# Linear attention and MoE mixer on one core: kv built transposed from split features, their column sums on GpSimd, four weight blocks reloaded in every batch

## The chip, the core and the metric

One core of a Trainium2 chip runs the whole kernel in one launch. The metric is the device time of that launch in microseconds. A core has TensorE (PE in the profile; its weight loads are PEld), VectorE (DVE), ScalarE (ACT), GpSimd (POOL) and SyncE (SP), which here only issues DMAs. TensorE reads SBUF and writes PSUM; VectorE and ScalarE read PSUM back.

## The reference

Eight batches, eight heads, 576 rows, head dimension 64, 128 features before the two signs:

```python
def phi(x):
    proj = np.einsum('bhsd,df->bhsf', x, w_phi)
    proj = proj - np.max(np.abs(proj), axis=-1, keepdims=True)
    return np.concatenate([np.exp(proj), np.exp(-proj)], axis=-1)
q_p, k_p = (phi(q), phi(k))
kv = np.einsum('bhsf,bhsd->bhfd', k_p, v)
z = np.sum(k_p, axis=2)
num = np.einsum('bhsf,bhfd->bhsd', q_p, kv)
den = np.einsum('bhsf,bhf->bhs', q_p, z)[..., None] + 1e-06
x = num / den          # then, with x as (batch, row, 512):
u = x + (xᵀ @ U @ V)ᵀ
out = u + np.maximum(u @ w_ch1, 0.0) @ w_ch2
```

The weights are float64 in memory and are turned into float32 on the chip.

## The kernel before

**Attention.** Work goes by pairs of heads: 4 pairs in a batch, 32 in all. Of the 576 rows, 512 go as four tiles of 128 (`NT`), and the last 64 of both heads as one "tail" tile. A `Pair` object has a step for each piece of the work: `s_project_k0` and `s_project_k1` (key features of each head, `kp`, 128 rows by 4 tiles by 256 features), `s_project_q0` and, inside `s_kv0_q1`, the second query head (query features `qp`, features by rows), `s_kv0_q1` and `s_kv1` (kv), `s_out0` and `s_out1` (queries times kv, then a division). In batches 0 and 1 (`split` false) everything runs in float32; from batch 2 on (`split` true, `SPLIT` is 2) the projections run in fp32r, a one-pass format, with operands split into a high and a low part. kv is float32 everywhere: `kv_tail` and `kv_main` hold the features as weights and stream v with a column of ones behind it (`vb`, 65 columns), so that column 64 of kv is z. `kv_done` copies kv from PSUM to SBUF. The features' maximum over 128 features is a VectorE reduction for k, and for q, whose features lie on partitions, a `partition_all_reduce` on GpSimd.

**MoE mixer.** A `Mixer` handles the 512 rows of a batch, and a ninth one the tails of all batches. It has 16 blocks f of 128 hidden columns: `hidden(f)` makes 12 fp32r matmuls of 512 columns into the one PSUM bank `ph`, ScalarE and VectorE split the result into `h_hi` and `h_lo` (L590, L591), and `add(f)` makes 12 more into the four banks `o`. All 32 weight tiles (`w1_f`, `w2_f`, high and low part, 512 KB each) stay in SBUF from their conversion (batches 0 and 1: `convert` on ScalarE, VectorE and, with `INT64_ADD`, GpSimd) to the end.

**Order.** The attention steps of the next pairs are woven with the 32 mixer chunks of the batch before: `mix` calls chunks between steps. A scheduler then sets the order of every engine's instructions by its own model of the time, and each engine keeps to that order. DMAs are all issued by SP, in its order. PSUM has 3 banks `at` for attention, 1 `ph` and 4 `o`. After the last pair only mixer chunks are left.

**What the change touches.** `load_weights`, `convert_block` and `place` name the weight tiles; `Pair.__init__` loads k and q; `project_k_split`, `project_q`, `kv_tail`, `kv_main`, `kv_done`, `out_main` and the steps `s_*` are those above; `hidden` and `add` are the mixer's.

## Time and profile before

| | |
|---|---|
| median of 3 runs | 1259.67 us (1258.68 to 1262.07) |
| profiled execution | 1257.95 us, span 1256.2 us |
| granted TensorE clock, mean | 0.991 |
| busy share of the span | PE 97%, PEld 83%, DVE 54%, ACT 43%, POOL 16% |
| chain that ended last | PE 84%, DVE 9%, ACT 4% |
| of that chain, by line | ph L585 30%, o L604 28%, kv L431 8%, xp L470 7% |

A row of a group of instructions reads: line, engine, operation, output <- inputs, shapes, count | busy us, mean ns of one | idle time of the engine before it and what ended that. Shapes are partitions x elements of one partition. A row of the order of time reads: start, duration, engine, line, operation, count. Matmuls are pipelined: each takes some 0.2 us longer than the step to the next, so a row's mean is not its price.

### The profile page before, as it was taken

How to read it: one execution, taken by the hardware profiler on the slowest of the kernel's cores; microseconds unless marked ns; L12 is line 12 of the kernel's file. 1: busy time of each engine (PE TensorE's matmuls, PEld its weight loads, DVE VectorE, ACT ScalarE, POOL GpSimd, SP SyncE). 2: the span in 40 equal slices, each digit the busy share in tenths (PEclk: the TensorE clock that was granted, in tenths of full speed). 3: DMA queues.
4: the chain of work that ended last, by engine and by line, in shares of the span. 5: the costliest groups of instructions: out<-in, count | busy, mean ns of one | idle time of the engine just before them, and what ended most of it. 6: DMA issues, size and time to landing. Idle time of an engine off the chain costs nothing.

```text
span 1256.2 us, 18188 instructions
## 1 busy us (share of the span) xinstructions
PE 1221.9 (97%) x6749; PEld 1044.6 (83%) x6749; DVE 680.5 (54%) x1489; ACT 541.6 (43%) x1151; POOL 204.0 (16%) x154
## 2 busy tenths in 40 slices
PE   7989998999999999999999999999999999999997
PEld 6877887888888888888888888888888888788886
DVE  5777889765566555565646556565646542212111
ACT  5766777444444444344434444344435430111110
POOL 3442444111110111011111111021101110000000
PEclk9899999999999999999999999999999999999999
DMA  5685111321132112311132112211222002100001
GB/s 125 210 254 176 65 28 29 100 63 27 32 87 62 25 29 58 93 30 29 29 100 62 23 34 64 80 30 27 45 78 63 17 1 88 67 1 1 34 1 33
DMA packets 188408, 75.42 MB, mean 60 GB/s; under 512 B 164256, under 2 KB 174752, under 8 KB 188192
## 3 DMA queue, kind: packets, MB, share of 16 engines
q1 hardware_dynamic: 188320, 74.27, 22.4%
q8 instruction: 53, 0.87, 0.3%
q14 instruction: 35, 0.29, 0.1%
HBM read 55.35 MB, written 18.87 MB: 59 GB/s over the span
## 4 chain that ended last, share of the span: by engine, by line
PE 84%; DVE 9%; ACT 4%; issue 1%; SPq 1%; DMA 1%; POOL 1%; DVEq 0%; ACTq 0%; POOLq 0%
PE ph L585 30%; PE o L604 28%; PE kv_ps L431 8%; PE xp L470 7%; PE pk L391 2%; PE pp L541 1%; DVE w L220 1%; PE kv_ps L424 1%; PE pq L414 1%; DVE uT_lo L228 1%; PE pt L573 1%; PE pq L415 1%; ACT w_ab L137 1%; ACT w_ab L138 1%; PE xpt L457 1%
## 5 line engine op out<-in xcount | busy, mean ns | idle before, releaser
L585 PE MATMUL ph<-uT_hi,w 128*128 128x512 f32 x1152 | 389.5, 398 | 2.3 <-ACT uT_hi L227 1.4
L604 PE MATMUL o<-w,h_hi 128*128 128x512 f32 x1152 | 330.7, 395 | 0.6 <-ACT h_hi L590 0.5
L585 PEld LDWEIGHTS ph<-uT_hi,w 128*128 128x128 f32 x1152 | 217.3, 189 | 48.9 <-ACT uT_hi L227 3.1
L604 PEld LDWEIGHTS o<-w,h_hi 128*128 128x128 f32 x1152 | 211.5, 188 | 42.5 <-ACT h_hi L590 1.2
L591 DVE SCALAR_TENSOR_TENSOR h_lo<-ph,h_hi 128x512 fp32r<-128x512 f32 x144 | 99.0, 687 | 256.5 <-ACT h_hi L590 256.1
L585 PE MATMUL ph<-uT_lo,w 128*128 128x512 f32 x576 | 227.3, 395 | 0.4 <-DVE uT_lo L228 0.4
L590 ACT ACTIVATE h_hi<-ph 128x512 fp32r<-128x512 f32 x144 | 85.9, 597 | 290.1 <-PE ph L585 281.3
L604 PE MATMUL o<-w,h_lo 128*128 128x512 f32 x576 | 198.0, 396 | 0.0
L355 POOL PARTITION_ALL_REDUCE qp<-qp x64 | 126.9, 1982 | 282.2 <-ACT qp L354 282.2
L431 PEld LDWEIGHTS kv_ps<-vb,kp 128*128 128x128 f32 x1024 | 126.0, 194 | 4.4 <-issue 1.4
L585 PEld LDWEIGHTS ph<-uT_lo,w 128*128 128x128 f32 x576 | 109.4, 190 | 22.2 <-DVE uT_lo L228 0.6
L470 PEld LDWEIGHTS xp<-kv,qp 128*128 128x128 f32 x1024 | 123.1, 192 | 5.4 <-ACT qp L358 1.0
L431 PE MATMUL kv_ps<-vb,kp 128*128 128x65 f32 x1024 | 125.1, 273 | 0.0
L470 PE MATMUL xp<-kv,qp 128*128 128x65 f32 x1024 | 123.2, 273 | 0.4 <-ACT qp L358 0.3
L604 PEld LDWEIGHTS o<-w,h_lo 128*128 128x128 f32 x576 | 105.6, 189 | 19.8
L355 POOL PARTITION_ALL_REDUCE qp_t<-qp_t x32 | 26.7, 834 | 433.6 <-ACT qp_t L354 433.6
L311 DVE TENSOR_TENSOR T<-raw,T 64x512 fp32r<-64x512 f32 x96 | 70.8, 737 | 29.3 <-ACT T L310 27.0
L345 ACT ACTIVATE kp<-kp 128x512 f32<-128x512 f32 x64 | 40.4, 632 | 103.8 <-DVE kp L342 71.5
L310 ACT CAST T<-raw 64x512 fp32r<-64x512 f32 x96 | 59.3, 618 | 29.2 <-PE pq L415 24.9
L357 ACT ACTIVATE qp<-qp 128x512 f32<-128x512 f32 x64 | 40.5, 632 | 66.2 <-DVE qp L356 65.8
L307 DVE STREAM_TRANSPOSE raw<-raw 128x512 f32<-128x512 f32 x48 | 34.1, 711 | 56.6 <-DMA raw<-in_q_dram 34.8
L146 POOL INT64_ADD w_ab<-w_ab x32 | 44.5, 1391 | 75.8 <-DVE w_ab L142 40.2
(127 smaller groups left out, 1371.3 us busy)
## 6 DMA issues: line engine op xcount, KB each, us to landing
words<-in_moe_w_ch_dram SPq DMA_DIRECT2D x32, 512.0 KB, 6.6
vb<-in_v_dram SPq DMA_DIRECT2D x64, 128.0 KB, 2.4
u_dram<-x SPq DMA_DIRECT2D x32, 256.0 KB, 2.6
st<-u_dram SPq DMA_DIRECT2D x16, 512.0 KB, 3.9
out_dram<-st SPq DMA_DIRECT2D x32, 256.0 KB, 2.2
raw<-in_k_dram SPq DMA_DIRECT2D x192, 32.0 KB, 1.9
raw<-in_q_dram SPq DMA_DIRECT2D x192, 32.0 KB, 1.9
raw<-in_k_dram SPq DMA_DIRECT2D x8, 256.0 KB, 2.9
```

What stands on the lines that cost most here:

```text
L146: nc.gpsimd.int64_add(a64, a64, b64)
L310: nc.scalar.copy(out=m[here, s, :], in_=x_[here])
L311: nc.vector.tensor_sub(m[there, s, :], x_[here], f32(m[here, s, :]))
L345: nc.scalar.activation(out=kp[:, :, 0:F], in_=kp[:, :, F:2 * F], func=AF.Exp)
L355: nc.gpsimd.partition_all_reduce(qp[:, 0, :], qp[:, 1, :], P, ReduceOp.absmax)
L357: nc.scalar.activation(out=qp[:, 0, :], in_=qp[:, 1, :], func=AF.Exp)
L431: nc.tensor.matmul(self.kv_v[:, f, g, :], kp[:, t, f * F:(f + 1) * F], self.vb[:, g, t, :], start=False, stop=(t == NT - 1), skip_group_ch ...
L470: nc.tensor.matmul(xv[:, c, :], qp[:, f, c * P:(c + 1) * P], self.kv[:, f, c // 2, :], start=(f == 0), stop=(f == 1))
L585: nc.tensor.matmul(ph, w1_part(f, l, c), r[:, c, :], start=(n == 0), stop=(n == 3 * NCC - 1))
L590: on_act = nc.scalar.activation(out=h_hi, in_=ph, func=AF.Relu)
L591: on_dve = nc.vector.scalar_tensor_tensor(out=h_lo, in0=ph, scalar=0.0, in1=f32(h_hi), op0=ALU.max, op1=ALU.subtract)
L604: nc.tensor.matmul(self.o[t], l[:, cs], w2_t[f][:, r, :], start=(f == 0 and n == 0), stop=(f == NFC - 1 and n == 2))
```

## The change

For the 24 pairs of batches 2 to 7:

- kv is built transposed. v is split into a high and a low part side by side (`v_parts`: 128 columns, which become the weights) and k's features into two parts (`k_parts`), and `kv_turned` streams both feature parts, 256 columns each in fp32r, past them: 8 matmuls a head. ScalarE and VectorE add the two halves of the result into `kvT`. At the head of the next turn of the loop, `kv_end` transposes kvT with two matmuls, adds it to the tail's kv, and puts z in.
- z no longer comes from the column of ones. `k_sums` adds the features over the partitions on GpSimd (128x1024 a head), SP stores one row of that in DRAM (`zd`), loads it back with features on partitions (`zc`, in pieces of 4 bytes), and `kv_end` reduces it on VectorE.
- SBUF for the parts comes from six weight tiles. Blocks 3, 7 and 11 no longer stay: after conversion, blocks 0, 3, 7 and 11 are written to DRAM (`kept`) from GpSimd's queue, and mixers 1 to 8 use block 0's place for the four in turn, reloading the next one behind the last use of the one before (`stream`, GpSimd's queue).

For the 8 pairs of batches 0 and 1, q is loaded in one DMA in place of four, and `project_q` makes each half from two matmuls that write every fourth element, so that a half is one head; `out_main` follows.

```diff
@@ weights
+    STREAM = (0, 3, 7, 11)
+    def place_of(n, f):
+        if f in STREAM[1:]:
+            return f"late{2 * STREAM.index(f) - 2 + n}"
+        return f"w{n + 1}_{f}"
+    def stream(n, g, f):
+        i = STREAM.index(f) + 1
+        to = STREAM[i % len(STREAM)]
+        if g == 0 or g == B and to == 0:
+            return
+        w = home.tile([P, 2, C], F32R, tag=place_of(n, 0), name=f"w{n + 1}_{to}_{g}")
+        nc.gpsimd.dma_start(out=w, in_=kept[to][:, n])
+        (w1_t, w2_t)[n][to] = w
...
+            if f in STREAM:
+                nc.gpsimd.dma_start(out=kept[f][:, n], in_=w)
@@ class Pair
-                elif n == 0:
+                else:
                     self.loaded = nc.sync.dma_start(
                         out=m, in_=src[b, hs, 0:SM, :].rearrange("h (p t) d -> p h (t d)", t=NT))
-                else:
-                    for g in range(2):
-                        for z in range(2):
...
+        def k_sums(self, g, kp):
+            zr = home.tile([P, NT, 2 * F], F32, tag="late2", name=f"zr{self.nm}_{g}")
+            nc.gpsimd.partition_all_reduce(zr, kp, P, ReduceOp.add)
...
+            nc.sync.dma_start(
+                out=self.zd[g:g + 1, :], in_=zr[0:1].rearrange("o t f -> o (t f)"))
+        def k_sums_turned(self):
+            self.zc = small.tile([P, 2, NT, 2], F32, tag="zc", bufs=2, name=f"zc{self.nm}")
+            nc.sync.dma_start(
+                out=self.zc.rearrange("p g t n -> p (g t n)"),
+                in_=self.zd.rearrange("g (t f) -> f (g t)", f=F))
+        def k_parts(self, g, kp):
...
+            nc.scalar.copy(out=hi, in_=kp)
+            nc.vector.tensor_sub(lo, kp, f32(hi))
+            return hi, lo
+        def kv_turned(self, g, parts):
+            kt = self.kt = self.ps(f"kt{g}_")
+            for t in range(NT):
+                for n in range(2):
+                    nc.tensor.matmul(
+                        kt[:, 0:2 * F], self.v_hl[:, g, t, :], parts[n][:, t, :],
+                        start=(t == 0 and n == 0), stop=(t == NT - 1 and n == 1))
...
+            nc.scalar.copy(out=self.kvT[r_, 1, :], in_=kt[D:2 * D, 0:2 * F])
+            nc.vector.tensor_add(self.kvT[r_, 0, :], kt[0:D, 0:2 * F], self.kvT[r_, 1, :])
+        def kv_end(self):
...
+            for f in range(2):
+                nc.tensor.transpose(
+                    out=kb[:, f * P:(f + 1) * P], in_=self.kvT[:, 0, f * F:(f + 1) * F],
+                    identity=ident)
+            self.kv_tail()
...
+            nc.vector.tensor_copy(out=self.kv, in_=self.kv_v)
+            nc.vector.tensor_add(
+                self.kv[:, :, :, 0:D], self.kv[:, :, :, 0:D],
+                kb.rearrange("p (f h d) -> p f h d", f=2, h=2))
...
         def project_q(self, s):
...
-                nc.tensor.matmul(pq, w_two[:, s, :], self.T[1], start=True, stop=True)
+                pv = pq.rearrange("f (p z i) -> f i z p", z=2, i=2)
+                for i in range(2):
+                    nc.tensor.matmul(
+                        pv[:, i], w_two[:, i, :],
+                        self.T[1][:, s * (SM // 2):(s + 1) * (SM // 2)], start=True, stop=True)
...
         def s_kv0_q1(self):
+            if self.split:
+                self.k_sums_turned()
+                self.kv_turned(0, self.parts0)
+                self.qp1 = self.project_q(1)
+                self.parts1 = self.k_parts(1, self.kp1)
+                return
@@ class Mixer, end of hidden(f) and of the matmuls of add(f)
+            if f in STREAM:
+                stream(0, self.g, f)
...
+            if f in STREAM:
+                stream(1, self.g, f)
@@ loop over pairs
+            cur.kv_end()
             far = Pair(*pairs[n + 2]) if n + 2 < len(pairs) else None
```

The built program shows where this puts the instructions. All places are in batch 5. TensorE before, around the first head's kv of the third pair (the names are output <- moving operand, weights; kv_ps is kv, pp the mixer's down projection, ph and o its blocks):

```order
L297 MATMUL tT_3_6880<-ident,t_r_3_6680 128x128
L424 MATMUL kv_ps_2_6916<-vt_90,kp_2_t 128x130 x2
L431 MATMUL kv_ps_2_6916<-vb_91,kp_2_0_6696 128x65
L541 MATMUL pp_0_6855<-xs_0_2_6820,u_all 128x256 x4
L541 MATMUL pp_0_6855<-xs_0_4_6825,u_all 128x256 x2
L431 MATMUL kv_ps_2_6916<-vb_91,kp_2_0_6696 128x65 x4
L585 MATMUL ph_5_6899<-uT_hi_6325,w_5_1376 128x512
```

TensorE now, where the second head's kv of that pair begins (kt is kv transposed, khi and klo the parts of the features):

```order
L709 MATMUL o_0_7123<-w_7_4_7414,h_lo_7_7665 128x512
L385 MATMUL kt_5_2_7491<-khi_2_1_7475,v_hl_2_7317 128x256
L709 MATMUL o_1_7124<-w_7_4_7414,h_lo_7_7665 128x512
L709 MATMUL o_2_7125<-w_7_4_7414,h_lo_7_7665 128x512
L709 MATMUL o_3_7126<-w_7_4_7414,h_hi_7_7664 128x512
L709 MATMUL o_3_7126<-w_7_4_7414,h_lo_7_7665 128x512
L385 MATMUL kt_5_2_7491<-klo_2_1_7476,v_hl_2_7317 128x256
L385 MATMUL kt_5_2_7491<-khi_2_1_7475,v_hl_2_7317 128x256
```

The 16 kv matmuls of 65 columns of a head have become 8 of 256 columns, which wait for the parts from ScalarE and VectorE.

The transposes of the same pair's kvT stand on TensorE 30 rows later, among the next pair's key projections (pk):

```order
L709 MATMUL o_0_7123<-w_8_1698,h_lo_8_7722 128x512
L709 MATMUL o_1_7124<-w_8_1698,h_lo_8_7722 128x512
L400 MATMUL kt_5_2_7491<-ident,kvT_2_7463 128x128 x2
L470 MATMUL pk_5_3_7565<-w_hl,T_5_3_7419 128x256 x2
L709 MATMUL o_2_7125<-w_8_1698,h_lo_8_7722 128x512
```

Before, kv ended with its last matmul of 65 columns; now these two stand between it and the first use.

GpSimd before, for the third and fourth pair of batch 5 (all are q's maxima; _t is the tail):

```order
L355 ISA qp_2_t<-qp_2_t 128x128
L355 ISA qp_2_0_6831<-qp_2_0_6831 128x512
L355 ISA qp_2_1_6930<-qp_2_1_6930 128x512
L355 ISA qp_3_t<-qp_3_t 128x128
L355 ISA qp_3_0_7131<-qp_3_0_7131 128x512
L355 ISA qp_3_1_7187<-qp_3_1_7187 128x512
```

GpSimd now, from the third pair's first query head on (zr are the sums over k's features, w the reloaded blocks 11 and 0 with their two tiles each):

```order
L211 DMA w_11_4_7668<-kept_107 128x1024
L434 ISA qp_2_0_7361<-qp_2_0_7361 128x512
L434 ISA qp_2_1_7469<-qp_2_1_7469 128x512
L211 DMA w_11_4_7783<-kept_107 128x1024
L353 ISA zr_3_0_7580<-kp_3_0_7564 128x1024
L434 ISA qp_3_t<-qp_3_t 128x128
L434 ISA qp_3_0_7698<-qp_3_0_7698 128x512
L353 ISA zr_3_1_7636<-kp_3_1_7620 128x1024
L211 DMA w_0_4_8030<-kept_104 128x1024
L434 ISA qp_3_1_7761<-qp_3_1_7761 128x512
L211 DMA w_0_4_8151<-kept_104 128x1024
```

Each reload waits for TensorE's last use of the block before it, and q's maxima stand behind reloads and sums.

SP before, for the loads of pair 1 of batch 5 (raw are the k and q loads, 8 DMAs each):

```order
L249 DMA raw_1_0_5968<-in_k_dram 32x8x32 x8
L269 DMA t_r_1_5986<-in_k_dram 64x2x64
L269 DMA t_r_1_5986<-in_q_dram 64x2x64
L283 DMA vt_96<-in_v_dram 64x64 x2
L280 DMA vb_97<-in_v_dram 128x4x64 x2
L249 DMA raw_1_1_5977<-in_q_dram 32x8x32 x8
```

SP now, for the same loads (zd is z's row in DRAM, zc its load back, here of the last pair of batch 4):

```order
L271 DMA raw_1_0_6412<-in_k_dram 32x8x32
L356 DMA zd_3_6170<-zr_3_0_6168 1x1024
L271 DMA raw_1_0_6412<-in_k_dram 32x8x32 x7
L283 DMA t_r_1_6430<-in_k_dram 64x2x64
L283 DMA t_r_1_6430<-in_q_dram 64x2x64
L356 DMA zd_3_6170<-zr_3_1_6224 1x1024
L271 DMA raw_1_1_6421<-in_q_dram 32x8x32 x2
L361 DMA zc_3_6332<-zd_3_6170 128x16x1
L271 DMA raw_1_1_6421<-in_q_dram 32x8x32 x6
```

The z stores, which wait for GpSimd, and the load back, which waits for the stores, stand inside the raw loads.

More of the change, by code (lines that the diff above doesn't have):

```diff
@@ L185, in tile_kernel @@
     LAST = NFC - 1
+    STREAM = (0, 3, 7, 11)
+    kept = {
+        f: dram.tile([P, 2, 2, C], F32R, name=f"kept{f}") for f in STREAM}
+    def place_of(n, f):
+        if f in STREAM[1:]:
+            return f"late{2 * STREAM.index(f) - 2 + n}"
+        return f"w{n + 1}_{f}"
     def place(f, dt, shape, name):
@@ L191, in place @@
             return both[:, 0], both[:, 1]
-        return [home.tile([P, *shape], dt, tag=f"w{n}_{f}", name=f"{name}_{n}") for n in (1, 2)]
+        return [home.tile([P, *shape], dt, tag=place_of(n, f), name=f"{name}_{n}") for n in (0, 1)]
+    def stream(n, g, f):
[6 more added lines that the diff above has]
+        (w1_t, w2_t)[n][to] = w
     def load_weights(f):
@@ L205, in convert_block @@
         if f < LAST:
-            w = home.tile([P, 2, C], F32R, tag=f"w{n + 1}_{f}", name=f"w{n + 1}_{f}")
+            w = home.tile([P, 2, C], F32R, tag=place_of(n, f), name=f"w{n + 1}_{f}")
             split_w((nc.scalar.copy, nc.vector.tensor_copy)[n], r, w)
+            if f in STREAM:
+                nc.gpsimd.dma_start(out=kept[f][:, n], in_=w)
         elif n == 0:
@@ L334, in k_tile @@
             return att.tile([P, ng, 2 * F], F32, tag=tag, bufs=bufs, name=f"kp{self.nm}_{n}")
+        def k_sums(self, g, kp):
+            zr = home.tile([P, NT, 2 * F], F32, tag="late2", name=f"zr{self.nm}_{g}")
+            nc.gpsimd.partition_all_reduce(zr, kp, P, ReduceOp.add)
+            if g == 0:
+                self.zd = dram.tile([2, NT * 2 * F], F32, tag="zd", bufs=2, name=f"zd{self.nm}")
+            nc.sync.dma_start(
+                out=self.zd[g:g + 1, :], in_=zr[0:1].rearrange("o t f -> o (t f)"))
@@ new lines, in k_sums_turned @@
+        def k_sums_turned(self):
[4 more added lines that the diff above has]
+        def k_parts(self, g, kp):
+            hi = home.tile([P, NT, 2 * F], F32R, tag=f"late{5 * g}", name=f"khi{self.nm}_{g}")
+            lo = home.tile([P, NT, 2 * F], F32R, tag="late1", name=f"klo{self.nm}_{g}")
+            nc.scalar.copy(out=hi, in_=kp)
+            nc.vector.tensor_sub(lo, kp, f32(hi))
+            return hi, lo
@@ new lines, in v_parts @@
+        def v_parts(self):
+            self.v_hl = home.tile([P, 2, NT, 2 * D], F32R, tag="late3", name=f"v_hl{self.nm}")
+            src = self.vb[:, :, :, 0:D]
+            nc.scalar.copy(out=self.v_hl[:, :, :, 0:D], in_=src)
+            nc.vector.tensor_sub(
+                self.v_hl[:, :, :, D:2 * D], src, f32(self.v_hl[:, :, :, 0:D]))
+        def kv_turned(self, g, parts):
[5 more added lines that the diff above has]
+                        start=(t == 0 and n == 0), stop=(t == NT - 1 and n == 1))
+            if g == 0:
+                self.kvT = home.tile([P, 2, 2 * F], F32, tag="late4", name=f"kvT{self.nm}")
+            r_ = slice(g * D, (g + 1) * D)
+            nc.scalar.copy(out=self.kvT[r_, 1, :], in_=kt[D:2 * D, 0:2 * F])
+            nc.vector.tensor_add(self.kvT[r_, 0, :], kt[0:D, 0:2 * F], self.kvT[r_, 1, :])
@@ new lines, in kv_end @@
+        def kv_end(self):
+            if not self.split:
+                return
+            kb = self.kt[:, 2 * F:4 * F]
+            for f in range(2):
[3 more added lines that the diff above has]
+            self.kv_tail()
+            self.kv = small.tile([P, 2, 2, D + 1], F32, tag="kv", bufs=1, name=f"kv{self.nm}")
+            nc.vector.tensor_copy(out=self.kv, in_=self.kv_v)
+            nc.vector.tensor_add(
+                self.kv[:, :, :, 0:D], self.kv[:, :, :, 0:D],
+                kb.rearrange("p (f h d) -> p f h d", f=2, h=2))
+            z = small.tile([P, 2, 2], F32, tag="z", bufs=2, name=f"z{self.nm}")
+            nc.vector.tensor_reduce(
+                out=z, in_=self.zc.rearrange("p g t n -> p n g t"), axis=AX.X, op=ALU.add)
+            nc.vector.tensor_add(
+                self.kv[:, :, :, D:D + 1], self.kv[:, :, :, D:D + 1], z.unsqueeze(3))
@@ L396, in project_k_split @@
                     out=k_w[:, ts_, :], in0=pk[:, :, 0, :], in1=kp[:, ts_, 0:F], op=ALU.add)
-            return self.k_features(g, k_w, kp)
+            self.k_features(g, k_w, kp)
+            self.k_sums(g, kp)
+            return kp
         def project_q_tail(self):
@@ L425, in kv_tail @@
                     self.kv_v[:, f, :, :], self.kpt[:, 0, f * F:(f + 1) * F], self.vt,
-                    start=(f == 0), stop=False, skip_group_check=True)
+                    start=(f == 0), stop=self.split and f == 1, skip_group_check=True)
         def kv_main(self, g, kp):
@@ L470, in out_main @@
                     nc.tensor.matmul(
-                        xv[:, c, :], qp[:, f, c * P:(c + 1) * P], self.kv[:, f, c // 2, :],
+                        xv[:, c, :], qp[:, f, c * P:(c + 1) * P],
+                        self.kv[:, f, c // 2 if self.split else s, :],
                         start=(f == 0), stop=(f == 1))
+            if not self.split:
+                h = self.h0 + s
+                self.normalize(s, xv, x[:, :, h * D:(h + 1) * D])
+                return
             xo = x.rearrange("p (s z) c -> p s z c", s=2)[:, s, :, self.h0 * D:(self.h0 + 2) * D]
@@ L493, in s_kv1 @@
         def s_kv1(self):
+            if self.split:
+                self.kv_turned(1, self.parts1)
+                return
             self.kv_main(1, self.kp1)
```

10 lines of the change are left out of this document (5 added, 5 removed).

## The prediction

> **What bounds the kernel now.** I read the page's head first, then the windows of the span, then the groups of instructions and the order of time on TensorE, and the waits last.
>
> ```profile
> span 1256.2 us, 18188 instructions
> PE 1221.9 (97%) x6749; PEld 1044.6 (83%) x6749; DVE 680.5 (54%) x1489; ACT 541.6 (43%) x1151; POOL 204.0 (16%) x154
> 0.00:62.80 62.80, 54.97 (x332) 45.34 (x333) 38.34 (x106) 42.13 (x96) 24.20 (x35) 0.95 0.58 167
> 188.40:219.80 31.40, 28.25 (x160) 23.58 (x158) 30.67 (x54) 24.76 (x50) 14.77 (x9) 1.00 0.16 29
> 400.00:970.00 570.00, 567.62 (x3248) 492.47 (x3248) 328.27 (x737) 251.93 (x550) 79.18 (x50) 1.00 0.22 50
> 970.00:1036.00 66.00, 66.00 (x386) 57.84 (x386) 31.82 (x81) 27.20 (x59) 9.46 (x6) 1.00 0.03 9
> L437 DVE COPY kv<-kv_ps 128x260 f32<-128x260 f32 x17 | 7.3, 427 | 13.5 <-PE kv_ps L431 13.5
> ```
>
> The window rows give the busy time of PE, PEld, DVE, ACT and POOL, then the granted clock and the DMA share. From 400 to 970 us TensorE lacks 2.4 us of 570, so there every matmul that goes is time that goes. The last row, of the same window, counts 17 head pairs, so a pair takes 570/17 = 33.5 us, and VectorE is busy for 328.27/17 = 19.3 us of it, ScalarE for 14.8. Only the first 62.8 us (7.8 us idle) and the weight conversion (188 to 220: VectorE busy 30.67 of 31.40, TensorE idle 3.2) are not bound by TensorE.
>
> **The kv matmuls.** The change touches the 24 pairs of batches 2 to 7.
>
> ```profile
> L431 PE MATMUL kv_ps<-vb,kp 128*128 128x65 f32 x1024 | 125.1, 273 | 0.0
> 402.66 2.57 PE L431 MATMUL kv_ps<-vb,kp 128*128 128x65 f32 x22
> 405.04 1.17 PE L604 MATMUL o<-w,h_hi 128*128 128x512 f32 x4
> 417.63 0.40 PE L391 MATMUL pk<-w_hl,T 128*128 128x256 f32 x2
> 417.86 0.40 PE L604 MATMUL o<-w,h_hi 128*128 128x512 f32 x1
> 435.70 0.96 PE L541 MATMUL pp<-xs,u_all 128*128 128x256 f32 x6
> 436.50 1.00 PE L431 MATMUL kv_ps<-vb,kp 128*128 128x65 f32 x8
> 402.11 0.27 PE L297 MATMUL tT<-ident,t_r 128*128 128x128 f32 x1
> 402.22 0.61 PE L424 MATMUL kv_ps<-vt,kp_t 128*128 128x130 f32 x4
> 440.75 0.48 PE L414 MATMUL pq<-T,w_hl 128*128 128x512 f32 x1
> 441.06 0.40 PE L415 MATMUL pq<-T,w_hl 128*128 128x512 f32 x1
> 441.30 0.63 PE L604 MATMUL o<-w,h_hi 128*128 128x512 f32 x2
> ```
>
> Matmuls overlap, so a price is the step from one start to the next. L431 has 1024 records for 32 pairs of 16 matmuls: an f32 matmul is two records. A record steps (405.04 - 402.66)/22 = 0.108 us. Removed: 24 x 32 = 768 records, 82.9 us. Added: 24 x 16 = 384 fp32r matmuls over 256 columns; fp32r rows of that shape step (417.86 - 417.63)/2 = 0.115 and (436.50 - 435.70)/6 = 0.133. I take 0.12, near the first, whose group is the purer one: 46.1 us (44.2 to 51.1). Two transposes of 128x128 a pair step like the one at 402.11, 0.11: 5.3 us. The first fp32r matmul behind f32 ones steps 0.31 (L414 at 440.75) and the next 0.24 (L415), 0.07 more; the order has 464 changes between the precisions before and 382 now, so 41 fewer of this direction: -2.9 us. Sum on TensorE: -82.9 + 46.1 + 5.3 - 2.9 = -34.4 us (-29 to -36).
>
> **What other engines get, a pair.**
>
> ```profile
> L591 DVE SCALAR_TENSOR_TENSOR h_lo<-ph,h_hi 128x512 fp32r<-128x512 f32 x144 | 99.0, 687 | 256.5 <-ACT h_hi L590 256.1
> L395 DVE TENSOR_TENSOR kp<-pk,kp 128x256 f32<-128x256 f32 x96 | 38.7, 417 | 13.2 <-ACT kp L394 13.0
> L354 ACT COPY qp<-pq 128x512 f32<-128x512 f32 x64 | 37.3, 583 | 14.9 <-PE pq L415 12.7 <-PE kv_ps L431 1.6
> L394 ACT COPY kp<-pk 128x256 f32<-128x256 f32 x96 | 34.5, 372 | 49.2 <-PE pk L391 48.9
> L355 POOL PARTITION_ALL_REDUCE qp<-qp x64: 1935/1939/2371, 14.1 to 1019.6; - x64
> 598.59 0.74 POOL L355 PARTITION_ALL_REDUCE qp_t<-qp_t  x1 [16.26 <-ACT qp_t L354]
> ```
>
> VectorE: 256 columns 0.417, 512 columns 0.687, so 1024 about 0.69 + 2 x 0.27 = 1.23. The low parts of k (2 x 1.23) and v (0.69), kvT (2 x 0.42), the add into kv (0.42) and two small ones (0.3) make 4.7 us: 24.0 of then 32.1 us, 75%. ScalarE: 2 x 1.0 for the high parts of k, 0.58 for v, 2 x 0.37: 3.3 us, 18.1 of 32.1. GpSimd: a reduction takes 0.74 at 128 columns and 1.94 at 512, so 3.5 at 1024, two of them: with q's, 2 x 1.94 + 0.74 + 7.0 = 11.6 us a pair, 36%. An addition in place of a maximum isn't in the trace; I bound it by 1.94 and 7 us. TensorE, the only full engine, hides all this as long as nobody is late.
>
> Late next would be the part behind ph: there is one ph bank, freed by L590 and L591, so VectorE can hold TensorE up if h_lo queues behind something that waits. Its new waits are for GpSimd (q's maximum now stands behind k's sums and the weight reloads), and, more often, for raw loads, which SP now issues between stores of z that wait for GpSimd.
>
> ```profile
> DVE raw L307 <- DMA raw<-in_q_dram: 34.8, 20, 3.5
> POOL qp L355 <- ACT qp L354: 282.2, 57, 9.3
> DVE qp L356 <- POOL qp L355: 4.4, 4, 2.3
> 425.41 0.40 PE L391 MATMUL pk<-w_hl,T 128*128 128x256 f32 x2
> 453.87 0.61 PE L457 MATMUL xpt<-kv,qp_t 128*128 128x130 f32 x4
> ```
>
> GpSimd mostly waits for its own input now (282.2 us for q alone), VectorE waits only 4.4 us in all for it, and raw loads already hold VectorE up for as much as 3.5 us without TensorE missing it. That cover I keep, in part: 0 to 1 us a pair lost (the conversion stretch loses 3.2 us of 31.4 with VectorE at 98%; at 75% it should be far less). I take 0.25 a pair, +6 us (0 to 24).
>
> z itself: the last key projection of the pair is at 425.41, and the first use of its kv at 453.87, 28 us. Between them stand an add like L395 for each half, a maximum, a subtraction and two exponentials over 512 columns of about L591's length (0.8 + 4 x 0.69 = 3.6 us), the sum (3.5), the store of z and its load back in 2048 pieces of 4 bytes. No row has such a load; by the rows of the next part, for 512 KB, the two take 8 to 13 us, 15 to 20 in all. Hidden, so zero, with 8 us for queues; if GpSimd is late by more than that, VectorE waits with h_lo behind it, which is rival A.
>
> **The reloads.** Eight of 512 KB a batch.
>
> ```profile
> words<-in_moe_w_ch_dram SPq DMA_DIRECT2D x32, 512.0 KB, 6.6
> st<-u_dram SPq DMA_DIRECT2D x16, 512.0 KB, 3.9
> 1113.39 2.72 PE ph L585 x12
> 1116.11 2.72 PE o L604 x12
> ```
>
> The shortest cover is in the last two mixers, where nothing lies between: hidden(1), add(0), hidden(2), add(1), 4 x 2.72 = 10.9 us from the last use of tile 0 to the first of tile 3; elsewhere 33.5/8 = 4.2 us a chunk, 16.8 us. Issue from GpSimd isn't in the trace; by the two DMA rows (3.9 to 6.6) and one 3.5 us reduction ahead of it, 4 to 10 us. Cost zero, with little to spare at the upper end. By the Trainium skill (DMA: Bandwidth & Descriptors, section on the anatomy of a SWDGE DMA) such a transfer takes about 2.0 us plus bytes/436 GB/s, estimated 3.2 us; the sum stays the same, and no run here shows that queue yet.
>
> **Start and conversion.**
>
> ```profile
> 1.23 1.99 SPq L260 DMA_DIRECT2D raw<-in_q_dram  x4
> 6.26 0.45 PE L297 MATMUL tT<-ident,t_r 128*128 128x128 f32 x1 [2.30 <-DMA t_r<-in_q_dram]
> 14.35 0.31 PE L297 MATMUL tT<-ident,t_r 128*128 128x128 f32 x1 [1.02 <-DMA t_r<-in_q_dram]
> L220 DVE TENSOR_TENSOR w<-w_ab,w x32: 644/692/1775, 62.5 to 235.7; 128x512 fp32r<-128x512 f32 x32
> L311 DVE TENSOR_TENSOR T<-raw,T x96: 684/686/1676, 187.0 to 992.3; 64x512 fp32r<-64x512 f32 x96
> ```
>
> q of batches 0 and 1 comes in one load in place of four (1.99 us), 1.5 us less of SP for each pair, and TensorE starts on the load behind it: -1.5 us at 6.26 and a part of 1.02 later (0 to -4). I take -2. The two half matmuls of q stream the same columns as the whole one: 0. Writing four tiles back, and pair (2,0)'s 4.7 us on a VectorE that is full from 188 to 220 us: 0 to +5, I take +2.
>
> Sum: -34.4 + 6 + 0 - 2 + 2 = -28.4 us, from the profiled execution's 1257.95 (span 1256.2): 1229.6. The median of the runs is 1259.67, 1.7 above, so I say 1231.
>
> **Rivals.**
> A, the cover is partly used up: waits of GpSimd and raw loads cost TensorE 0.6 to 1.25 us a pair in place of 0.25, 8 to 24 us more: 1239 to 1255. For it: VectorE rises to 75% and its queue is in order; against: 570 us with 2.4 us idle in spite of all waits now.
>
> B, VectorE becomes the bound and it gets slower. Instructions with two operands in SBUF are held up by a reduction on GpSimd: the slowest T is 1.676 us, 1.0 above its usual 0.686, and L220 likewise. If each of some ten such instructions a pair (T, q, the low parts) were held for 1 us, VectorE would need 34 of 32 us; TensorE then idles as at 188 to 220, 3.2 us in 31.4, over 24 pairs of 32.1 us 78 us: about 1309. It decides from 1.2 us a pair above my 0.25 on, 28 us in all, where nothing of the gain is left. Against: T's median is its minimum, so most aren't held. The Trainium skill (SBUF — State Buffer, section Who interferes with whom) says that the port pair of VectorE and GpSimd is locked for a whole instruction; by that rule a 3.5 us reduction holds such an instruction for up to 3.5 us, and the sum would be B's 1309 in place of 1231. The trace agrees that they collide, but shows at most half of a 1.94 us reduction.
>
> C, the reload is late: each of the eight mixers 1 to 8 then waits on tile 3, at 20 us of latency 2 x 9.1 + 6 x 3.2 = 37 us: 1268; at 19 us the gain is about gone. Against: 3.9 to 6.6 us in the rows.
>
> D, nothing gained: with new weights each time a 256-column matmul steps 0.20, or everything is lost to waits to within 4 us: 1260. Against: 0.133, the dearest step of such a run.
>
> **Numbers.** Forecast (1216 to 1238: the ends of the TensorE sum and of the start, -7, and some 0.3 us a pair of waits more, +7) 0.58; A 0.21; D 0.05; B 0.13; C 0.03. The range, 1216 to 1255, holds the first two. A measurement tells 0.3%, 3.8 us, from no change: faster 0.79, same 0.05, slower 0.16.
>
> **What would show it.** Right: the kv matmuls' 16 records a pair step 0.12, TensorE's busy time is some 34 us less, and the window of the middle batches stays within a few us of full. Wrong: TensorE idle before ph with h_lo as releaser (A, B); two-operand rows of VectorE at twice their time (B); TensorE waiting for a GpSimd DMA (C); kt steps of 0.2 (D); or a sum on GpSimd far over 3.5 us.

## The result and the profile after

The changed kernel takes 1401.1 us (median of four runs, 1393.8 to 1402.5) against 1259.2 for the kernel before: 1.112 times as long (95% interval 1.109 to 1.114). The forecast was 1231 us, faster. It was wrong in sign, and the time is far outside its range.

From the page of the changed kernel: its span, the busy time of the engines, the chain's shares, and then one row of the windows, the stretch of middle batches that the prediction read.

```profile
span 1398.7 us, 18303 instructions
PE 1256.1 (90%) x6443; PEld 1054.9 (75%) x6445; DVE 922.5 (66%) x1681; ACT 621.8 (44%) x1271; POOL 536.4 (38%) x272
PE 34%; DVE 32%; ACT 10%; DMA 8%; SPq 8%; issue 5%; POOL 2%; DVEq 0%; ACTq 0%; POOLq 0%
...
400.00:970.00 570.00, 495.47 (x2507) 414.34 (x2506) 415.62 (x731) 253.66 (x523) 246.59 (x96) 0.93 0.30 70
```

In the middle batches TensorE was idle for 2.4 us of 570; now it is idle for 74.5, and the granted clock is 0.93 in place of 1.00, so its busy time too holds slower matmuls. Of the chain that ended last, 32% lies on VectorE. No engine is full: the loss consists of waits, and of slower matmuls behind them.

The groups that grew, in the changed kernel (columns: busy us, mean ns of one, idle time before and its releasers), then the row of the kernel before that answers to L631, and two rows of the view by tile (shortest, median and longest, in ns).

```profile
L353 POOL PARTITION_ALL_REDUCE zr<-kp x48 | 295.0, 6145 | 196.7 <-ACT kp L425 167.2
L370 DVE TENSOR_TENSOR klo<-kp,khi 128x1024 fp32r<-128x1024 f32 x48 | 143.6, 2991 | 32.9 <-ACT khi L369 26.8
L325 DVE TENSOR_TENSOR T<-raw,T 64x512 fp32r<-64x512 f32 x96 | 79.8, 831 | 12.6 <-ACT T L324 9.7
L631 DVE TENSOR_TENSOR xs<-x,xs 128x256 fp32r<-128x256 f32 x64 | 67.2, 1090 | 9.7 <-ACT xs L630 9.6
```
```profile
L528 DVE TENSOR_TENSOR xs<-x,xs 128x256 fp32r<-128x256 f32 x64 | 29.1, 490 | 11.3 <-ACT xs L527 11.1
```
```profile
L370 DVE TENSOR_TENSOR klo<-kp,khi x48: 1181/3130/5553, 216.9 to 1172.2; 128x1024 fp32r<-128x1024 f32 x48
L353 POOL PARTITION_ALL_REDUCE zr<-kp x48: 6107/6114/6548, 216.4 to 1172.9; - x48
```

A sum on GpSimd takes 6.1 us, not 3.5. The same subtraction `klo` takes 1.18 us at its shortest, as the prediction estimated, and 5.55 at its longest. Sorted by what GpSimd did meanwhile, the nine `klo` that ran clear of GpSimd average 1.21 us and the 36 that lay at least 60% beside GpSimd's work 3.58; `xs` goes from 0.42 to 1.52. Operations with one operand in PSUM didn't change: the longest `h_lo` beside GpSimd's work is 0.69 us.

The moment at which a held operation ends is the clearest sign of what holds it. Of the `klo` that started during a sum, 28 took over 20% more than alone, and 27 of them ended 0.50 us before the sum's recorded end, whether they had started 0.5 or 4.2 us into it (the other one started in the sum's last 0.1 us and met the next reduction). The ten held `xs`, which need 0.8 us less, all ended 1.30 us before it. So each was let go 1.7 us before the sum's recorded end, as were four subtractions of q's maximum; those that started in its last 1.4 us were not held by it.

One such place in the order of time (start, duration, engine, line; in brackets the idle time before, and its releaser):

```profile
706.73 6.11 POOL L353 PARTITION_ALL_REDUCE zr<-kp  x1 [5.14 <-ACT kp L425]
706.82 1.89 PE L555 MATMUL xp<-kv,qp 128*128 128x65 f32 x16
707.67 4.66 DVE L370 TENSOR_TENSOR klo<-kp,khi 128x1024 fp32r<-128x1024 f32 x1 [1.74 <-ACT khi L369]
712.78 0.42 DVE L534 TENSOR_TENSOR x<-xp,den 128x256 f32<-128x256 f32 x1
713.35 0.30 PE L484 MATMUL pqt<-tail_T,w_hl 128*128 128x128 f32 x1 [2.95 <-DVE x L534]
713.60 3.26 PE L555 MATMUL xp<-kv,qp 128*128 128x65 f32 x16
```

The sum starts, `klo` starts behind it and takes 3.5 us more than alone, VectorE's queue (the division into `x`) stands behind it, and TensorE is idle for 2.95 us. Then it pays once more: 16 matmuls of L555 take 3.26 us where 16 such took 1.89 at 706.82, before the wait. The granted clock is 0.5 from 714.07 to 720.89 us.

The trace of the changed kernel has 27 such stretches at half the clock, 145 us in all. Before each but the last, which lies at the program's end, TensorE had been idle for at least 1.5 of the 3.4 us ahead of it. In these stretches matmuls of 512 columns are 0.43 us apart (median), elsewhere 0.23. That the idle time brings the lower clock on is what the order of events suggests; no run sets the two apart.

The longest waits of TensorE in total name VectorE (total us, times, longest of one); the wait of VectorE for z stands below them, then the row of the reloads, whose last figure is the time from issue to landing:

```profile
PE pt L676 <- DVE x L661: 21.9, 8, 5.5
PE pqt L484 <- DVE x L534: 18.8, 6, 4.0
PE ph L688 <- DVE h_lo L694: 15.2, 13, 1.4
```
```profile
DVE z L410 <- DMA zc<-zd: 41.9, 15, 4.7
```
```profile
w<-kept POOLq DMA_DIRECT2D x62, 512.0 KB, 4.1
```

No matmul waits for a reload, and the matmuls of kv step as forecast, with a median of 0.12 us:

```profile
733.39 0.28 PE L385 MATMUL kt<-klo,v_hl 128*128 128x256 f32 x1
733.51 0.28 PE L385 MATMUL kt<-khi,v_hl 128*128 128x256 f32 x1
```

### The profile page after: what moved, and what is told of

It is laid out like the page before. It is cut to its first block, busy times and chain, and to the rows that moved or that the text cites. A ratio compares the mean times of both kernels' runs of the same rounds, so it can differ in the third digit from the quotient of the medians.

```text
span 1398.7 us, 18303 instructions
## 1 busy us (share of the span) xinstructions
PE 1256.1 (90%) x6443; PEld 1054.9 (75%) x6445; DVE 922.5 (66%) x1681; ACT 621.8 (44%) x1271; POOL 536.4 (38%) x272
## 4 chain that ended last, share of the span: by engine, by line
PE 34%; DVE 32%; ACT 10%; DMA 8%; SPq 8%; issue 5%; POOL 2%; DVEq 0%; ACTq 0%; POOLq 0%
PE ph L688 12%; PE o L709 11%; DVE klo L370 8%; SPq L271 6%; DVE T L325 4%; PE xp L555 3%; DVE xs L631 2%; DVE mk L419 2%; DMA zc<-zd 2%; DVE h_lo L694 2%; DVE kp L474 2%; DVE kp L421 2%; DMA raw<-in_q_dram 2%; ACT khi L369 2%; ACT kp L424 1%
## 5 line engine op out<-in xcount | busy, mean ns | idle before, releaser
L353 POOL PARTITION_ALL_REDUCE zr<-kp x48 | 295.0, 6145 | 196.7 <-ACT kp L425 167.2
L709 PE MATMUL o<-w,h_hi 128*128 128x512 f32 x1152 | 338.3, 416 | 5.7 <-ACT h_hi L693 5.6
L709 PEld LDWEIGHTS o<-w,h_hi 128*128 128x128 f32 x1152 | 225.2, 201 | 54.9 <-ACT h_hi L693 9.2
L709 PE MATMUL o<-w,h_lo 128*128 128x512 f32 x576 | 188.4, 393 | 0.0
L211 POOL DMA_DIRECT2D w<-kept x62 | 34.3, 553 | 355.6 <-PE pk L470 144.5
L370 DVE TENSOR_TENSOR klo<-kp,khi 128x1024 fp32r<-128x1024 f32 x48 | 143.6, 2991 | 32.9 <-ACT khi L369 26.8
L555 PE MATMUL xp<-kv,qp 128*128 128x65 f32 x1024 | 136.8, 291 | 12.6 <-DVE kp L474 12.6
L555 PEld LDWEIGHTS xp<-kv,qp 128*128 128x128 f32 x1024 | 134.8, 208 | 17.3 <-DVE kp L474 13.7
L325 DVE TENSOR_TENSOR T<-raw,T 64x512 fp32r<-64x512 f32 x96 | 79.8, 831 | 12.6 <-ACT T L324 9.7
L631 DVE TENSOR_TENSOR xs<-x,xs 128x256 fp32r<-128x256 f32 x64 | 67.2, 1090 | 9.7 <-ACT xs L630 9.6
```

The source lines that it names most:

```text
L325: nc.vector.tensor_sub(m[there, s, :], x_[here], f32(m[here, s, :]))
L353: nc.gpsimd.partition_all_reduce(zr, kp, P, ReduceOp.add)
L370: nc.vector.tensor_sub(lo, kp, f32(hi))
L555: nc.tensor.matmul(xv[:, c, :], qp[:, f, c * P:(c + 1) * P], self.kv[:, f, c // 2 if self.split else s, :], start=(f == 0), stop=(f == 1))
L631: nc.vector.tensor_sub(xs[:, 1, :], src, f32(xs[:, 0, :]))
L709: nc.tensor.matmul(self.o[t], l[:, cs], w2_t[f][:, r, :], start=(f == 0 and n == 0), stop=(f == NFC - 1 and n == 2))
```

## The experiments

The theories. **Port** (later "lock"): a VectorE operation with two operands in SBUF stands still while a GpSimd reduction runs. **Load**: VectorE and ScalarE just have too much to do. **Queue** (later also "lateness"): z's chain, or what stands behind it on SP's or GpSimd's queue, comes too late. **Reload**: the four weight tiles come late. **Cover**: kv's cheaper products no longer hide the waits at a batch's end. All times are single runs unless more are given; single runs of the kernel before, on the same chips, lay between 1256.7 and 1262.2.

**The sum taken out**

```diff
-            nc.gpsimd.partition_all_reduce(zr, kp, P, ReduceOp.add)
...
-                out=self.zd[g:g + 1, :], in_=zr[0:1].rearrange("o t f -> o (t f)"))
+                out=self.zd[g:g + 1, :], in_=kp[0:1].rearrange("o t f -> o (t f)"))
```

> The changed kernel without the sum of k's features on GpSimd: the store of z takes a row of the features themselves, so z is left out of the result, and everything else (parts, kt matmuls, transposes, store and load back of z, reloads) stays. Port theory (the 6.1 us sum reads SBUF and holds VectorE's instructions with two SBUF operands; VectorE runs late, TensorE idles): 1225 to 1245 us, klo near 1.2 us in place of 3.0. Queue theory (the long sum makes q's maxima and z late): also 1225 to 1245. Load theory (VectorE's 4.7 us of new work a pair is too much by itself): over 1330. Reload theory (GpSimd's queue and DMAs for the weight tiles): over 1330.

Measured: 4655.85 us, which no theory had. The row of TensorE's first work, products on zeros ahead of any data:

```profile
1.23 7.95 PE L812 MATMUL busy<-zeros 128*128 128x512 bf16 x6 [1.23 <-DVE zeros L807]
```

Six of them take 7.95 us; in the changed kernel 2.74. So TensorE was slower by a factor of about 3 from the first instruction, at a granted clock of 1.0 in the records, before anything of the change could matter; `klo` on VectorE took its usual 1.22 us. The run says nothing of the sum, and I repeated it (the step of these products in the changed kernel is 0.43 us, not the 0.22 that the text below says):

> The kernel of the first experiment a second time: the sum over partitions on GpSimd is gone, zd is stored from kp's first row, so the output lacks the true z; everything else of the change stays (the store and the load that turn z, the kv in feature layout, the reloads, q's whole loads). In the first run TensorE needed 1.3 us for each of the six 128x512 products on zeros that open the program, where after needs 0.22 between starts, so nothing of the change could have come into it yet. If that was a disturbance of that one run, the time is now 1220 to 1260 us by the lock theory (VectorE's klo back to 1.2 us everywhere, xs to 0.42) and by the lateness theory alike (no 6.1 us in z's chain); by the load theory (VectorE has too much to do) it stays above 1300. If 4656 us comes again, the cause is in this program and not in the chip's state.

Measured: 1259.4 us, with `klo` at 1.22 us on average and `xs` at 0.51.

```profile
PE 1197.4 (95%) x6443; PEld 1021.4 (81%) x6445; DVE 781.2 (62%) x1681; ACT 619.9 (49%) x1271; POOL 246.8 (20%) x224
L368 DVE TENSOR_TENSOR klo<-kp,khi 128x1024 fp32r<-128x1024 f32 x48 | 58.8, 1224 | 29.7 <-ACT khi L367 28.1
```

So the sum is worth 141 us of the changed kernel's time. On TensorE these are 82 us more of idle time and 59 us more of busy time for the same matmuls (the table at the end of the experiments). VectorE's busy time also differs by 141 us, but that is a coincidence as far as the runs show, since TensorE did not wait for all of it. Load falls as the main cause: VectorE still does all its added work here. What made the first run slow stays open. Also open was why 1259 is still 28 us above the forecast; see "batch ends" below.

**GpSimd as busy, but without reading** (a sum over 128x128 and four memsets; z is not the true one)

```diff
-            nc.gpsimd.partition_all_reduce(zr, kp, P, ReduceOp.add)
+            nc.gpsimd.partition_all_reduce(zr[:, 0, 0:F], kp[:, 0, 0:F], P, ReduceOp.add)
+            for _ in range(4):
+                nc.gpsimd.memset(zr, 1.0)
```

> GpSimd is kept busy for about as long as by the sum, without reading SBUF for most of it: each sum is replaced by one over 128 columns (0.7 to 1 us) and four memsets of 128x1024, together some 5 to 6 us; z is left out. Port theory: klo back to 1.2 to 1.6 us, 1230 to 1265 us. Queue theory: as slow as the changed kernel, 1370 to 1400.

Measured: 1325.6 us. Its groups, and its longest wait of SP's queue:

```profile
L355 POOL MEMSET zr<- 128x1024 f32 x192 | 185.4, 965 | 8.4
L372 DVE TENSOR_TENSOR klo<-kp,khi 128x1024 fp32r<-128x1024 f32 x48 | 58.5, 1219 | 45.0 <-ACT khi L371 44.6
...
SPq L358 <- POOL zr L355: 345.1, 31, 19.7
```

GpSimd works 4.95 us for each head, and `klo` runs at its own 1.22 us: the memsets, which only write SBUF, don't hold it. The Trainium skill (SBUF — State Buffer, section Who interferes with whom) says just that: two SBUF operands contend with a GpSimd instruction that reads SBUF, not with one that only writes it. But 66 us over the kernel without a sum are left, with VectorE's operations no slower than there (`xs` 0.45 against 0.51 us, `T` 0.74 against 0.72): GpSimd's time costs in a second way (the last experiment).

**A shorter reduction** (the maximum in place of the sum; z is not the true one; the instructions stand in the same order as in the changed kernel)

```diff
-            nc.gpsimd.partition_all_reduce(zr, kp, P, ReduceOp.add)
+            nc.gpsimd.partition_all_reduce(zr, kp, P, ReduceOp.absmax)
```

> The sum becomes a maximum of absolute values of the same 128x1024, in the same instruction order; z is left out. By the rows of q's maxima (0.74 us at 128 columns, 1.94 at 512) it takes 3.5 us if the operation sets the price, and 6.1 if the size does. Port theory and queue theory: with 3.5 us the time falls by about half of what is lost, to 1290 to 1340; with 6.1 it stays at 1400. Load and reload theories: 1400 either way.

Measured: 1302.6 us.

```profile
L353 POOL PARTITION_ALL_REDUCE zr<-kp x48 | 171.2, 3568 | 192.2 <-ACT kp L425 141.9
L370 DVE TENSOR_TENSOR klo<-kp,khi 128x1024 fp32r<-128x1024 f32 x48 | 87.5, 1823 | 34.2 <-ACT khi L369 29.8
```

The maximum takes 3.57 us, which is the 3.5 that the prediction worked out for the sum: from the maxima of q it had the price of a maximum, and an addition costs 1.72 times that. 124 us less of GpSimd are 98 us less of time, with every engine's instructions in the same order: nothing but the length of the reduction differs. Even at 3.5 us the kernel would have been slower than before, so the mis-sized sum alone does not explain the forecast's error.

**The reloads alone**, in the kernel before (blocks 0, 3, 7 and 11 written back once and reloaded; nothing else of the change)

> The kernel before with the reload of weight tiles alone (blocks 0, 3, 7, 11 written to DRAM and reloaded by mixers 1 to 8 on GpSimd's queue; kv, z and the loads of q as before). Port and queue theories: 1255 to 1266 us. Reload theory: 1290 or more, with TensorE waiting for the tiles or GpSimd's maxima late.

Measured: 1256.1 us, the kernel before beside it 1257.1. A reload lands in 4.3 us. Reload falls, and the cost of zero was right.

**z not waited for** (sum, store and load stay; kv's last column is added from a constant, so z is not the true one)

```diff
-                out=z, in_=self.zc.rearrange("p g t n -> p n g t"), axis=AX.X, op=ALU.add)
...
+                self.vb[:, :, 0:2, D:D + 1])
```

> The sum on GpSimd, its store and its load stay as they are, but nothing waits for them on VectorE: z is added from a constant (v's column of ones) in place of zc, so the output lacks the true z. By the lock theory the 6.1 us sums still stop klo (3 us mean) and xs (1.1 us mean), and at most the 42 us that VectorE waited for zc can go: 1350 to 1395 us. By the lateness theory (z's chain of sum, store and load comes too late for kv) the time falls to 1230 to 1290 us with klo's mean still at 3 us.

Measured: 1388.7 us, with `klo` at 2.89 us on average. VectorE's wait of 42 us for z was worth some 12 us (5 against the fastest run of the changed kernel); lateness of z falls as the main cause.

**The same sum in four instructions**

```diff
-            nc.gpsimd.partition_all_reduce(zr, kp, P, ReduceOp.add)
+            for t in range(NT):
+                nc.gpsimd.partition_all_reduce(zr[:, t, :], kp[:, t, :], P, ReduceOp.add)
```

> The same sum in four instructions of 128x256 in place of one of 128x1024; the same numbers come out. By the lock theory (VectorE's operations with two operands in SBUF wait until the running GpSimd instruction lets go) klo under GpSimd falls from 3.6 us to 1.5 to 2.8, since it waits for a quarter at most, and the time falls by 20 to 110 us to 1290 to 1380, though GpSimd works as long as before (four times 1.6 to 2 us against 6.1). By the load theory and by the lateness theory the time is 1390 to 1430 us, as GpSimd's sums last as long or longer.

Measured: 1329.2 us.

```profile
L354 POOL PARTITION_ALL_REDUCE zr<-kp x192 | 366.9, 1983 | 217.0 <-ACT kp L426 184.8
L371 DVE TENSOR_TENSOR klo<-kp,khi 128x1024 fp32r<-128x1024 f32 x48 | 65.9, 1372 | 27.2 <-ACT khi L370 19.6
```

GpSimd works 72 us longer, on the same numbers, and the kernel is 72 us faster: what counts is how long one instruction keeps VectorE out. It speaks for the lock, since load and lateness could only have grown.

**z without GpSimd** (a reduction over kp's four tiles on VectorE, four products with the column of ones on TensorE; no store, no load; four runs)

```diff
-            nc.gpsimd.partition_all_reduce(zr, kp, P, ReduceOp.add)
+            nc.vector.tensor_reduce(
+                out=self.zs[:, g, :], in_=kp.rearrange("p t f -> p f t"), axis=AX.X, op=ALU.add)
...
+                        self.kv_v[:, f, g, D:D + 1], self.zs[:, g, f * F:(f + 1) * F],
+                        self.vb[:, g, 0, D:D + 1],
```

> z without GpSimd and without the two transfers: VectorE adds kp's four tiles (one tensor_reduce of 128x1024 to 128x256 for a head, estimated 1.2 us from klo alone, 1.21), and TensorE adds four products with v's column of ones to kv's tail (four at 0.11 us). The rest of the change stays. Priced on the forecast's terms: 1231 us, plus 24 x 0.44 = 10.6 on TensorE, plus 2.4 us of VectorE a pair that is hidden if the lock was the cause: 1230 to 1265 us. By the load theory (VectorE's work for a pair, 24 of 32 us and now 26, is what stalls TensorE) it is above 1300 us.

Measured: 1285.2 us, 1.020 times the kernel before (1.017 to 1.024). The expectation missed two prices: the reduction takes 2.02 us, not 1.2, and a float32 product is two records on TensorE, so z costs some 20 us there, not 10.6. The same with two additions in place of the reduction:

> The kernel with z on VectorE and TensorE (1285 us), with two additions (128x512 and 128x256, estimated 0.69 and 0.42 us from the additions of the same sizes) in place of the one reduction, which measured 2.00 us: 0.9 us less for a head, 43 us less of VectorE over the program; the same z. If VectorE's work in a pair still costs time there at the rate of the last step (from no z, 1259, to this z, 1285, with 96 us more on VectorE and 10.6 on TensorE: 26 us), half of the added VectorE work goes and 7 to 12 us with it: 1271 to 1279 us. If that 26 us is TensorE's 10.6 and the batch ends, nothing: 1281 to 1290.

Measured: 1276.4 us, 9 less, inside the first of the two ranges; the additions take 0.76 and 0.44 us. It is one run, so how much of VectorE's work counts in full isn't settled by it.

**Batch ends.** In the kernel without the sum TensorE still waits in one place, in the order of time at the end of a batch:

```profile
385.08 0.71 DVE L321 STREAM_TRANSPOSE raw<-raw 128x512 f32<-128x512 f32 x1 [2.88 <-DMA raw<-in_q_dram]
386.29 2.47 DVE L726 TENSOR_TENSOR st<-st,o 128x512 f32<-128x512 f32 x4
388.68 1.28 DVE L659 TENSOR_TENSOR x<-x,vp 128x512 f32<-128x512 f32 x2
389.41 1.97 PE L674 MATMUL pt<-ident,x 128*128 128x128 f32 x8 [5.42 <-DVE x L659]
```

VectorE waits 2.88 us for q's load, other work and `x` stand behind it in its order, and the next mixer's transposes wait 5.42 us for `x`. Two experiments on the kernel without the sum (so without the true z), and a control on the kernel before. First, two chunks of the mixer more held back for the end of a batch, `HELD = 4` made 6:

> The kernel without the sum (1259.4 us) with one number changed: six mixer chunks in place of four are held back for the end of each batch (HELD), about 5.6 us more of TensorE work there. The kernel without the sum still stands 28 us above the forecast, and its TensorE waits 26 us for VectorE's x at the six ends of batches (PE pt from DVE x, 5.4 us the longest). Theory cover: kv's one-pass products took away what TensorE did at the end of a batch, so the wait of VectorE for q's load is uncovered there; then two chunks more cover it and the time falls by 10 to 28 us, to 1231 to 1249, with that wait below 10 us. Theory rate: VectorE's and ScalarE's added work slows every pair alike, and the time stays 1255 to 1265 us.

Measured: 1238.3 us, 21 less; TensorE's wait for `x`, first without and then with the two chunks:

```profile
PE pt L674 <- DVE x L659: 25.9, 6, 5.4
PE pt L674 <- DVE x L659: 10.6, 6, 1.8
```

The control, the kernel before with HELD 6:

> The kernel before with the same number changed (HELD 6). Control: its TensorE never waits for x at a batch's end (no such row among its waits), so by the theory cover nothing is to be had there: 1255 to 1265 us. If it gains as much as the kernel without the sum does, the held chunks are a gain of their own and say nothing of the change.

Measured: 1258.8 us (beside it 1261.2): nothing to be had there beyond what two single runs differ by. So the change uncovered the wait at the batch ends. Whether kv's cheaper products did it, as the theory says, or VectorE's added work, which also makes `x` later, isn't set apart. Then the order of the steps that fill the end of a batch:

```diff
-                    fill = [nxt.s_project_q0, far.transposes, nxt.s_kv0_q1, nxt.s_kv1]
+                    fill = [nxt.s_project_q0, nxt.s_kv0_q1, far.transposes, nxt.s_kv1]
```

> The kernel without the sum, with the next-but-one pair's transposes moved behind the first kv product in the list of steps that fill a batch's end, so that VectorE meets the wait for q's load one step later. By the theory that VectorE stands in its own order in front of a late load with x queued behind, the wait of TensorE for x falls from 26 us to below 13 and the time by 8 to 25 us, to 1234 to 1251; if the wait only moves to another row, 1255 to 1265.

Measured: 1252.4 us, 7 less, the wait 9.6 us. The sign and the wait are as expected, the gain just short of the range.

And the changed kernel itself with HELD 6, sum and true z included:

> The changed kernel, sum on GpSimd and all, with HELD 6. By the lock theory VectorE stands still in every pair (24 times two sums of 6.1 us), which 5.6 us of TensorE work at a batch's end cannot cover: the time falls by no more than the 21 us that the kernel without the sum gained, to 1378 to 1401 us. By the theory that the sum only lengthens the batch ends, it falls to 1300 or lower.

Measured: 1390.8 us. Held chunks win 10 us here: the sum's price lies mostly in every pair, not at the batch ends.

**Is there a version that wins?** z by two additions with HELD 6 (four runs):

> z by two additions on VectorE and four products on TensorE (1276 us) with HELD 6; the outputs are those of the reference. From the gain of the kernel without the sum (21 us): 1276 - 21 = 1255, and a little lower if the 12 us that are left over TensorE's own 10.6 for z also lay at the batch ends: 1243 to 1258 us, against about 1259 for the kernel before. If it stays above 1265, VectorE's work is the bound in every pair and not only at the ends.

Measured: 1272.4 us, 1.011 times the kernel before (1.009 to 1.013), above the expected range. The expectation would lay that on VectorE's work in every pair. By the traces, of the 34 us between this kernel and the one without the sum and with HELD 6, 25 are busy time of TensorE, z's products and slower matmuls, and 8 its idle time. z's products alone take this much on TensorE (192 records of about 0.105 us from start to start, 20.1 us):

```profile
L398 PE MATMUL kv_ps<-vb,zs 128*128 128x1 f32 x192 | 23.4, 243 | 0.0
```

A version with eight chunks held gave no time: its instructions wait for each other in a circle. With z in two fp32r parts (one-pass products; four runs), and with the batch end's order changed as well (four runs):

> HELD 6 and z by two additions on VectorE, as in the 1272 us kernel, but the sums are split into a high and a low fp32r part (one copy on ScalarE, about 0.6 us, one subtraction on VectorE, about 0.7 us a pair), and eight one-pass products of two columns make z in place of four two-pass ones of one. If a one-pass product costs 0.058 us (the shortest of the fp32r projections of the tail, pkt and pqt), TensorE's z falls from 20.1 to 24 x 8 x 0.058 = 11 us: 1260 to 1266 us if VectorE is not the bound, 1272 to 1285 if VectorE's added 17 us count in full; if such a product costs 0.1 us like the float32 passes, 1270 to 1275.

> The same with the transposes of the next-but-one pair moved behind the first kv product at a batch's end, which brought 7 us to the kernel without the sum. Theory cover: 4 to 8 us less than the run before, 1253 to 1262; if six held chunks cover the ends already, the same within 4 us.

Measured: 1283.2 us (1.019, 1.017 to 1.021) and 1281.6 us (1.019, 1.016 to 1.021). A one-pass product with two columns steps 0.112 us (median), like a float32 record, so TensorE saves nothing: the steps behind z's products add up to 24.0 us, against 20.1. What makes up the rest of the 11 us isn't known; it is busy time of TensorE, which waits no longer than in the 1272 us kernel (idle 51.1 us against 50.5). The order is worth nothing that can be told here. The order alone, on z in float32:

> The 1272 us kernel (z in float32, HELD 6) with the same move of the transposes. Theory cover: its TensorE still waits 17.3 us for x at seven places; the wait falls below 10 us and the time to 1263 to 1269 us. If the wait is only shifted: 1270 to 1275.

Measured: 1267.9 us in one run, 4.5 less, in the range of the theory cover, but with a wait of 15.6 us where that theory had it below 10; the gain is not explained by the wait. It is the best version with the true z, and none beats the kernel before.

**GpSimd's second price.** In the kernel with the memsets SP waited 345 us for `zr`. Here GpSimd issues that store itself (z is not the true one):

```diff
-            nc.sync.dma_start(
+            nc.gpsimd.dma_start(
                 out=self.zd[g:g + 1, :], in_=zr[0:1].rearrange("o t f -> o (t f)"))
```

> The kernel with a 128x128 sum and four memsets in place of the sum (1325.6 us; its output lacks the true z), with the store of zd issued by GpSimd itself, behind the memsets, in place of SP. SP then waits for zr no more; for zd's landing it still waits before the load of zc. Theory SP queue: the 66 us over the kernel without a sum (1259) were raw and st loads held back behind that store; most of it goes: 1262 to 1290 us. Theory GpSimd's time: q's maximum and the reloads come late because GpSimd is busy; then it stays at 1310 to 1340.

Measured: 1289.6 us, 36 less, at the very end of the range for SP's queue. SP's wait for `zr` is gone, and a part of it is now the wait for the store to land, ahead of the load that turns z:

```profile
SPq L363 <- DMA zd<-zr: 89.1, 12, 37.8
```

So about half of the 66 us was SP's queue behind the store of z. The other 30 have no experiment of their own: the wait above, GpSimd's time, or the order, which the scheduler makes anew for each of these kernels.

**What TensorE lost.** Idle is the span less the busy time; the last column is the busy time that lies in stretches at half the clock (us, profiled executions).

| kernel | idle | busy | of it at half clock |
|---|---|---|---|
| before | 34 | 1222 | 20 |
| changed | 143 | 1256 | 127 |
| without the sum | 60 | 1197 | 38 |
| maximum in place of the sum | 90 | 1211 | 47 |
| sum in four instructions | 100 | 1227 | 82 |
| memsets | 85 | 1239 | 97 |
| memsets, store on GpSimd's queue | 67 | 1221 | 66 |

The matmuls are the same in the last six rows, so their busy times differ by how fast TensorE ran. For the sum's 141 us the idle time gives 82 and the busy time 59; at half speed, 127 less 38 us make an estimate of 45 of these 59. Of the memsets' 66 us, 25 are idle time and 41 busy time.

## Why the prediction was wrong, step by step

- **The kv matmuls, -34.4 us: right.** In the kernel without the sum and with HELD 6 the 384 steps add up to 46.2 us (46.1 said), and TensorE's busy time is 28 us less than before (29 to 36 said). That kernel runs in 1238.3 us, 21 under the kernel before, but it lacks z, which costs some 20 us where TensorE makes it.
- **What other engines get: one term mis-sized.** `klo` alone is 1.21 us (1.23 said), the high part of k 1.05, v's 0.74 and 0.62: right. The sum on GpSimd is 6.1 us and not 3.5. The prediction saw that no addition was in the trace and bounded it by 7, but let the bound touch only z's chain and not VectorE.
- **The stalls, 0.25 us a pair: the step that failed.** The sum asked who waits for GpSimd's results, and found 4.4 us. VectorE operations held by GpSimd's reading of SBUF stood in a rival only, and matmuls slowed behind a wait nowhere. Measured, the sums on GpSimd cost 141 us over 24 pairs, 5.9 us a pair: 82 us of idle TensorE and 59 us of slower matmuls. Some 72 to 75 us of the 141 go with the lock (the quarters and the memsets), the rest with a GpSimd that is busy.
- **Rival B had the mechanism,** at 0.13. Its 78 us of waits, taken from the conversion stretch, are near the lock's share, but the whole time is 92 us above its 1309. The argument against it failed: T's median being its minimum told of a GpSimd that was busy for 16% of the span, and now is for 38%. The bound from the trace, half of a 1.94 us reduction, could not hold for a longer one; the longest `klo` was held 4.4 us in a 6.1 us sum. The rule of the Trainium skill that the prediction weighed there (SBUF — State Buffer, Who interferes with whom: locked for the whole instruction) is nearer to what was seen than the row on which the prediction decided. It is not exact here: the held operations were let go 1.7 us before the sum's recorded end.
- **Rival A is real too**: the forecast had 6 us for all waits, and of the 28 us between it and the kernel without the sum, 21 came back with two held chunks.
- **z's chain hidden: nearly right.** Its lateness cost some 12 us, not zero. What was missed is SP: the store of z waits for GpSimd, and raw loads and `st` stand behind it on SP's queue, some 36 us in the kernel with the memsets.
- **Reloads at zero: right** (1256.1 against 1257.1 us), and the landing of 4.1 to 4.3 us lies at the lower end of the 4 to 10 forecast. The estimate by the Trainium skill (DMA: Bandwidth & Descriptors, Anatomy of one DMA — SWDGE (gpsimd) path), 3.2 us, is about 1 us short of it.
- **Start and conversion** weren't tested apart.

The prices don't add up exactly: kernels differ in order too. For the sum's 141 us the runs give 72 for the length of one instruction (quarters) and about 66 that are left where GpSimd is busy without reading. 36 of these 66 went with SP's queue. z's wait, 12 us, was measured in the changed kernel and may lie in either part.

## What to carry to other kernels

Before work is moved to an idle GpSimd, ask which VectorE operations with two operands in SBUF will run at that time, and price each at what is left of the GpSimd instruction, not at its own length; here cutting the instruction into pieces gave back half of the loss at no saving of work. A price read from one kind of reduction isn't the price of another: measure the addition itself. A wait of TensorE can cost more than its length: read the granted clock behind it. And when a change takes time off the bound engine, look for the places where that time had hidden someone else's wait, here the ends of the batches.

## What the runs showed of the hardware

- `partition_all_reduce` on 128x1024: 6.11 us for an addition, 3.57 for a maximum of absolute values; an addition over 128x256 takes 1.98, over 128x128 1.09.
- A VectorE operation with two operands in SBUF that starts in a 6.11 us sum is let go 1.7 us before the sum's recorded end, wherever in the first 4.2 us it started (41 of 41). GpSimd's memset of 128x1024, 0.97 us, did not slow `klo` (1.22 us). VectorE's one-operand reduction (128x1024 to 128x256) took 2.00 us clear of GpSimd and 2.04 beside it.
- A matmul with one float32 column costs two records of 0.105 us, as much as one with 65 columns (0.107); with two fp32r columns it is one record of 0.112 (median).
- In the changed kernel the granted clock fell to half 27 times, for 145 us in all; 26 times TensorE had been idle for at least 1.5 of the 3.4 us before. The step of 512 columns was 0.43 us there, else 0.23.
- In one run TensorE was slower by a factor of about 3 from its first instruction, at a recorded clock of 1.0; the same kernel run again was not. The cause is open.
